# Gated linear attention with routed experts on one core: the decay matrices of chunks 2 to 5 from two 64x64 triangles and a product of two factors

## The chip, the cores and the metric

One core of a Trainium2 chip runs the whole program, in one launch. The metric is the device time of one execution in microseconds (us); lower is better. The engines are TensorE (PE in the profile, its weight loads PEld), VectorE (DVE), ScalarE (ACT), GpSimd (POOL) and SyncE (SP), whose queue issues most DMAs. Each works through its own instructions in program order; semaphores order them against each other.

## The reference, cut to what matters

```python
# attention: batch 4, heads 8, seq 768, head_dim 40
for t in range(S):
    m_new = np.maximum(f_gate[:, :, t] + m, i_gate[:, :, t])
    f_stab = np.exp(f_gate[:, :, t] + m - m_new)
    i_stab = np.exp(i_gate[:, :, t] - m_new)
    m = m_new
    C = f_stab * C + i_stab * np.einsum('bhd,bhe->bhde', vt, kt)
    n = f_stab * n + i_stab * kt
    h_tilde = np.einsum('bhde,bhe->bhd', C, qt)
    denom = np.maximum(np.abs(np.einsum('bhd,bhd->bh', n, qt)), 1.0)
    y[:, :, t] = sigmoid(o_gate[:, :, t]) * h_tilde / denom
# then 8 experts 320 -> 1024 -> 320, one per token (the best logit), weighted by its probability
# then one dense block 320 -> 2048 -> 320 for all 3072 tokens
```

The attention is a linear recurrence with a scalar decay `f_stab` per head and token. Over a chunk of 128 tokens it becomes a few matrix products, in which the weight of key token s for query token t is the product of the decays from s + 1 to t. That triangle of products, 128x128 for each head, is what the change computes in another way.

## The kernel before, in words

The attention is cut into 24 units: chunk c (128 tokens, 6 of them) by batch b (4 of them), unit u being chunk u // 4 and batch u % 4. All 8 heads of a batch are done at once. The loop over u is written out by hand, and what stands in the program first comes first on its engine; there is no planner in it.

For unit u the work is this. `fload` (L264) brings the chunk's decays of 8 heads, 1024 numbers, to all 128 partitions of `fb`. `scan` (L358) runs VectorE's scan over them, multiply and add with a shifted identity: row s of the result `pm` is the running product that starts at token s, which is the triangle. `scores_mm` (L392) makes the scores `sp` of 8 heads on TensorE, `scores_w` (L402) multiplies them by `pm` to `wm`, and `pv` (L453) multiplies `wm` by the values into `op`. `kweigh` (L383, GpSimd) weighs the keys by the last column of `pm`, and `state` (L407) makes of them the product `dC`, which `state_up` (L423, VectorE) adds to the state `Cst`, decayed by `state_decay` (L417, three instructions on ScalarE). `inter` (L437) multiplies the queries by the state. `epilogue1` and `epilogue2` join both parts in `num` and make the denominator `dn`; `finish` (L495) multiplies by the gate `sg` on GpSimd and leaves the token rows `x`. Two units later `route_t` (L503) transposes `x` (into `pr`, copied to `xT` by ScalarE), and `route_l` (L533) makes the logits, which VectorE copies to `logit_all`. `route_hot`, `route_rank` and `route_cnt` find, for 4 units at a time, the slot of each token with its expert; `scatter` (L613, GpSimd, from unit 10 on) writes the rows there.

On GpSimd the order in a unit is `sg` and `x` of unit u - 2, `vp_in` (the weighted values) of unit u + 1, `kw` of unit u + 1, a row scatter. On TensorE it is `sp` of u, `op` of u - 1, `pr` of u - 2, `dC` of u, `ip` of u, the logits of u - 2. In the last chunk (units 20 to 23) there is no `kw`, `dC`, `Cst` decay or update. From unit 10 on halves of expert weights are split into two parts beside it (ScalarE L105 and L118, VectorE L110, L111 and L121).

The gates of all 32 heads stand on 32 partitions. Chunks 0 and 1 are prepared at the start, chunks 2 to 5 in units 0 to 5 (`gates_m`, `gates_x`, `gates_exp_f`, `gates_z`, `gates_e`, `gates_pe`). `put_dec` writes the decays to DRAM, from where `fload` spreads them.

The attention is followed by the experts and the dense block, in which TensorE multiplies 128x128 weight blocks in fp32 split into two fp32r parts.

## Time and profile before

| | us |
|---|---|
| median of 3 runs (lowest, highest) | 760.16 (759.28, 760.32) |
| the profiled execution | 759.01 |
| its span, first to last instruction | 757.3 |

| engine | busy us | share of the span |
|---|---|---|
| TensorE (PE) | 712.0 | 94% |
| VectorE (DVE) | 538.7 | 71% |
| ScalarE (ACT) | 345.2 | 46% |
| GpSimd (POOL) | 232.4 | 31% |

The shares are means over two stages with different limits. The page's picture of the span in 40 slices of 18.9 us each shows VectorE at 8 to 9 tenths in the first ten slices (the attention) and at 4 to 7 after them, TensorE at 6 to 9 in the first ten and at 9 tenths or more in nearly all the others. A row of the order of time is an instruction, or several alike merged: its start, how long from the first start to the last end, engine, line, operation, what it writes from what, shapes and count; in brackets how long the engine stood idle before it and whose end released it.

### The profile page before, as it was taken

Reading aid. Unit: us, or ns where it says so; the run is one execution under the profiler, and the core shown is the slowest. Engines: PE = TensorE matmul, PEld = TensorE weight load, DVE = VectorE, ACT = ScalarE, POOL = GpSimd, SP = SyncE. Lnnn points to the kernel's source line nnn. Section 1 sums busy time; section 2 is a strip of 40 time slices with the busy share of each in tenths; the row PEclk is TensorE's granted clock in tenths of the full one; section 3 lists DMA queues with packets and bytes.
Section 4 is the critical chain, followed back from the end, with each engine's and each line's share of the span. In section 5 each row is a group of like instructions: output and inputs, shape, how many; then the busy total and the mean of one; then the engine's idle time right before and its main releaser. Section 6 shows DMA issues by size and latency. Waiting matters only on the chain.

```text
span 757.3 us, 13220 instructions
## 1 busy us (share of the span) xinstructions
PE 712.0 (94%) x4708; PEld 669.0 (88%) x4708; DVE 538.7 (71%) x1082; ACT 345.2 (46%) x806; POOL 232.4 (31%) x346
## 2 busy tenths in 40 slices
PE   7697888878999999999999999999999999999995
PEld 6697888878888999999998888998889988899994
DVE  7889999998499989898976765544544554445542
ACT  4344243332566666676645443333333343334442
POOL 4563476785343333455401003003003003002011
PEclk9889999999999999999999999999999999999998
DMA  6979887672559777877732121211211101101000
GB/s 188 314 244 300 265 268 237 205 256 77 165 198 234 234 203 188 233 209 232 250 82 80 27 59 46 42 33 40 40 41 36 37 26 35 43 1 46 11 19 18
DMA packets 69913, 99.57 MB, mean 131 GB/s; under 512 B 31218, under 2 KB 56082, under 8 KB 69842
## 3 DMA queue, kind: packets, MB, share of 16 engines
q1 hardware_dynamic: 66770, 90.79, 40.6%
q0 software_dynamic: 3072, 7.89, 2.9%
q8 instruction: 38, 0.62, 0.3%
q14 instruction: 33, 0.27, 0.1%
HBM read 77.53 MB, written 17.19 MB: 125 GB/s over the span
## 4 chain that ended last, share of the span: by engine, by line
issue 42%; PE 23%; POOL 5%; DVE 2%; DMA 1%; ACT 0%; POOLq 0%; SPq 0%; ACTq 0%
PE acc L1131 12%; PE hp L138 10%; POOL out_dram L1176 3%; POOL xr L1282 2%; PE xt L1055 1%; DMA xr<-y 1%; DVE w L121 0%; POOL gap L1178 0%; DVE hs L1105 0%; DVE xl L1057 0%; DVE w L111 0%; DVE fr L1200 0%; POOLq L1626 0%; DVE xl L1073 0%; ACT hs L1444 0%
## 5 line engine op out<-in xcount | busy, mean ns | idle before, releaser
L1131 PE MATMUL acc<-wout,hhl 128*128 128x320 f32 x1152 | 187.0, 309 | 0.0
L1131 PEld LDWEIGHTS acc<-wout,hhl 128*128 128x128 f32 x1152 | 175.9, 188 | 7.4
L1116 DVE TENSOR_TENSOR sg<-hp,sg 128x512 f32<-128x512 f32 (+1 forms) x112 | 68.8, 614 | 93.5 <-ACT sg L1115 93.1
L138 PE MATMUL hp<-xh,win 128*128 128x512 f32 (+1 forms) x560 | 131.0, 364 | 0.0
L1118 DVE TENSOR_TENSOR hhl<-sg,hhl 128x512 fp32r<-128x512 f32 (+1 forms) x112 | 71.3, 637 | 70.2 <-ACT hhl L1117 70.2
L1176 POOL DMA_INDIRECT out_dram<-o,tokd x24 | 24.0, 1001 | 312.4 <-ACT o L1160 308.7
L1115 ACT ACTIVATE sg<-hp 128x512 f32<-128x512 f32 (+1 forms) x112 | 60.4, 539 | 124.6 <-PE hp L138 124.6
L1131 PE MATMUL acc<-w,hs 128*128 128x320 f32 x636 | 104.9, 310 | 2.0 <-ACT hs L1104 1.0
L138 PEld LDWEIGHTS hp<-xh,win 128*128 128x128 f32 x560 | 93.9, 188 | 11.5 <-ACT xh L1321 0.2
L1131 PEld LDWEIGHTS acc<-w,hs 128*128 128x128 f32 x636 | 96.8, 188 | 4.4 <-DVE hs L1105 1.9
L1117 ACT CAST hhl<-sg 128x512 fp32r<-128x512 f32 (+1 forms) x112 | 62.6, 559 | 80.1 <-DVE sg L1116 80.1
L138 PE MATMUL hp<-xl,win 128*128 128x512 f32 (+1 forms) x336 | 85.7, 363 | 0.0
L110 POOL TENSOR_TENSOR w<-r,w 128x256 fp32r<-128x256 f32 x58 | 47.7, 824 | 106.6 <-ACT w L105 94.2
L138 PEld LDWEIGHTS hp<-xl,win 128*128 128x128 f32 x336 | 58.8, 189 | 10.9 <-DVE xl L1322 0.2
L138 PE MATMUL hp<-xh,w 128*128 128x440 f32 (+6 forms) x320 | 66.8, 338 | 0.0
L400 PE MATMUL sp<-qT,kblk 120*128 120x128 f32 x384 | 51.9, 292 | 11.9 <-DVE wm L405 11.9
L400 PEld LDWEIGHTS sp<-qT,kblk 120*128 120x128 f32 x384 | 48.2, 204 | 16.7 <-DVE wm L405 14.6
L360 DVE TENSOR_TENSOR_SCAN pm<-fb,ident_h 128x1024 f32<-128x1024 f32 x23 | 57.3, 2492 | 5.2 <-DMA fb<-dec 2.0
L138 PEld LDWEIGHTS hp<-xh,w 128*128 128x128 f32 x320 | 51.4, 189 | 1.7
L1104 ACT ACTIVATE hs<-hp 128x440 fp32r<-128x440 f32 (+6 forms) x64 | 30.2, 472 | 41.5 <-PE hp L138 40.1
L463 PE MATMUL op<-vp_in,wm 128*128 128x128 f32 (+1 forms) x368 | 44.6, 275 | 0.0
L463 PEld LDWEIGHTS op<-vp_in,wm 128*128 128x128 f32 x368 | 43.5, 194 | 0.0
(304 smaller groups left out, 1082.8 us busy)
## 6 DMA issues: line engine op xcount, KB each, us to landing
r<-in_w_dram SPq DMA_DIRECT2D x32, 704.0 KB
fb<-dec SPq DMA_DIRECT2D x23, 512.0 KB
kvo<-in_kvo_dram SPq DMA_DIRECT2D x24, 480.0 KB
c<-in_wio_dram SPq DMA_DIRECT2D x16, 704.0 KB
rows<-zt SPq DMA_DIRECT2D x8, 640.0 KB
qT<-in_qT_dram SPq DMA_DIRECT2D x24, 180.0 KB
xr<-y SPq DMA_DIRECT2D x5, 640.0 KB
kblk<-in_kT_dram SPq DMA_DIRECT2D x48, 60.0 KB
```

The lines of the kernel that those rows point to most:

```text
L110: eng.tensor_tensor(out=t[:, 3 * P:5 * P].rearrange("p (c f) -> p c f", c=2), in0=r1[:, 0:2], in1=hif[:, 0:2], op=ALU.subtract)
L138: nc.tensor.matmul(hp, a, b, start=(i == 0), stop=(i == len(seq) - 1))
L360: nc.vector.tensor_tensor_scan(out=pm[u].rearrange("p h t -> p (h t)"), data0=fb[u].rearrange("p h t -> p (h t)"), data1=ident_h.rearrange ...
L400: nc.tensor.matmul(sp[:, h - hs.start], kblk[u % NLD][0:KR, h // 3, h % 3, :], qT[u][0:KR, h // 3, :], start=True, stop=True)
L463: nc.tensor.matmul(ops[:, h * NW:h * NW + n], wm[u][:, h], vp_in[u % NLD][:, h * DV:h * DV + n], start=True, stop=True)
L1104: nc.scalar.activation(out=hh, in_=hp, func=AF.Relu)
L1115: nc.scalar.activation(out=sg, in_=hp, func=AF.Sigmoid, scale=1.702)
L1116: nc.vector.tensor_tensor(out=g, in0=hp, in1=sg, op=ALU.mult)
L1117: nc.scalar.copy(hh, g)
L1118: nc.vector.tensor_tensor(out=hl, in0=g, in1=hh.bitcast(F32), op=ALU.subtract)
L1131: nc.tensor.matmul(acc_t[blk][i], hl if j == 2 else hh, w[:, DM:2 * DM] if j == 1 else w[:, 0:DM], start=(first and j == 0), stop=(last an ...
L1176: sc = nc.gpsimd.indirect_dma_start(out=out, out_offset=bass.IndirectOffsetOnAxis(ap=tokd[:, ti:ti + 1], axis=0), in_=o[:, i], in_offset=None)
```

## The change

For chunks 2 to 5 (units 8 to 23) the triangle of 128 tokens is put together from three blocks of 64. `fload` brings the decays of the first 64 tokens to the upper 64 partitions of `fb` and those of the last 64 to the lower, so that one scan of 512 elements makes both triangles. It writes to a PSUM tile `tri`; ScalarE copies the first triangle into `pm` (L429). The square between them is a product of two factors, the decays from s to token 63 and those from token 64 to t, made on TensorE (`far_mm`, one product of K = 96: for 8 heads the factors' high parts and the low parts of each, against zeros for the other heads) into the upper half of the same PSUM tile; `far_out` copies square and second triangle into `pm` (L444). The gates therefore stand on 96 partitions, three copies of the 32 heads, each loaded by a DMA of its own.

The factors are made once: `masks` in unit 1, `factors` in `gates_e` in unit 4, `suffix` in two parts in units 5 and 6, and their spreading over heads and batches (`spread_b`, `spread_a`) at the ends of units 5 and 6. `far_mm` stands behind `inter` in a unit, `far_out` and `kweigh` behind `state_decay`. Besides, `pv` multiplies 96 columns at a time instead of 128, `pm` is two fixed tiles, and a later tile takes the place of a `wm` tile instead of a `pm` tile.

```diff
-        ig = ap1.tile([BH, S], F32, name="ig")
-        fg = ap1.tile([BH, S], F32, name="fg")
-        nc.sync.dma_start(out=fg, in_=f_gate.rearrange("b h s -> (b h) s"))
-        nc.sync.dma_start(out=ig, in_=i_gate.rearrange("b h s -> (b h) s"))
+        R3, HP, CH = 3 * BH, P // 2, 2
+        ig = ap1.tile([R3, S], F32, name="ig")
+        fg = ap1.tile([R3, S], F32, name="fg")
+        for t, g in ((fg, f_gate), (ig, i_gate)):
+            for a in range(3):
+                nc.sync.dma_start(out=t[a * BH:(a + 1) * BH], in_=g.rearrange("b h s -> (b h) s"))
...
+            else:
+                fb[u] = fb[u][:, 0:H * HP]
+                for a in range(2):
+                    src = dec[1][2 * (c - CH) + a, b * H:(b + 1) * H].rearrange("h t -> (h t)").unsqueeze(0)
+                    nc.sync.dma_start(out=fb[u][a * HP:(a + 1) * HP], in_=src.to_broadcast([HP, H * HP]))
...
+        def masks():
+            v = ident[0:R3, 0:R3].rearrange("k (a b h) -> k a b h", b=B, h=H)
+            nc.vector.tensor_reduce(out=hmask, in_=ident[0:R3, 0:R3].rearrange("k (a h) -> k h a", h=H), axis=AX.X, op=ALU.add)
+            nc.vector.tensor_reduce(out=bmask, in_=v.rearrange("k a b h -> k b a h"), axis=AX.XY, op=ALU.add)
+            for a in range(2):
+                nc.vector.tensor_copy(id2[a * HP:(a + 1) * HP],
+                                      ident[a * HP:(a + 1) * HP, a * HP:(a + 1) * HP].unsqueeze(1).to_broadcast([HP, H, HP]))
+        def suffix(second):
+            if not second:
+                nc.gpsimd.memset(facA[:, :, HP - 1:HP], 1.0)
+                nc.gpsimd.tensor_copy(facA[:, :, 0:HP - 1], fz[:, CH:NCH, 1:HP])
+            k = 8 if second else 1
+            while k < (HP if second else 8):
+                nc.vector.tensor_tensor(out=facA[:, :, 0:HP - k], in0=facA[:, :, 0:HP - k], in1=facA[:, :, k:HP], op=ALU.mult)
+                k *= 2
+            if not second:
+                return
+            nc.scalar.copy(fac["fa"], facA)
+            lo = slice(BH, 2 * BH)
+            nc.vector.tensor_tensor(out=fac["fa"][lo], in0=facA[lo], in1=fac["fa"][lo].bitcast(F32), op=ALU.subtract)
+        def factors():
+            late = est[:, CH:NCH, HP:P]
+            nc.scalar.copy(fac["fb"], late)
+            lo = slice(2 * BH, R3)
+            nc.vector.tensor_tensor(out=fac["fb"][lo], in0=late[lo], in1=fac["fb"][lo].bitcast(F32), op=ALU.subtract)
+            nc.vector.tensor_tensor(out=late, in0=late, in1=est[:, CH:NCH, HP - 1:HP].to_broadcast([R3, NCH - CH, HP]), op=ALU.mult)
+        def spread_a():
+            for b in range(B):
+                nc.scalar.mul(lhsA[:, b], fac["fa"].bitcast(F32), bmask[:, b:b + 1])
+        def spread_b(h0, h1):
+            for h in range(h0, h1):
+                nc.scalar.mul(rhsB[:, :, h], fac["fb"].bitcast(F32), hmask[:, h:h + 1])
...
         def scan(u):
-            pm[u] = wk.tile([P, H, P], F32, tag="pm", name="pm")
+            pm[u] = pmb[u % 2]
+            if units[u][1] >= CH:
+                t = tri_t[u] = ps_t.tile([P, H, HP], F32, tag="pt", name="tri")
+                nc.vector.tensor_tensor_scan(out=t.rearrange("p h t -> p (h t)"), data0=fb[u], data1=id2.rearrange("p h t -> p (h t)"),
+                                             initial=0.0, op0=ALU.mult, op1=ALU.add)
+                nc.scalar.copy(pm[u][0:HP, :, 0:HP], t[0:HP])
+                return
...
+        def far_mm(u):
+            b, c = units[u]
+            if c >= CH:
+                nc.tensor.matmul(tri_t[u][0:HP].rearrange("p h t -> p (h t)"), lhsA[:, b, c - CH],
+                                 rhsB[:, c - CH].rearrange("k h t -> k (h t)"), start=True, stop=True)
+        def far_out(u):
+            if units[u][1] >= CH:
+                nc.scalar.copy(pm[u][:, :, HP:P], tri_t.pop(u))
...
-                n = min(2, H - h) * NW
+                n = NW + NW // 2 if h < H - 1 else NW
...
                 if ok(u + 1):
                     vprime(u + 1)
-                    kweigh(u + 1)
+                    if units[u + 1][1] < CH:
+                        kweigh(u + 1)
...
                 inter(u)
+                if ok(u + 1):
+                    far_mm(u + 1)
...
                 state_decay(u)
+                if ok(u + 1) and units[u + 1][1] >= CH:
+                    far_out(u + 1)
+                    kweigh(u + 1)
```

The order on ScalarE in unit 11, before (`vp_in` is a column of the weighted values, `Cst` the state of a batch, `w` a split weight):

```order
L381 COPY vp_in_118<-ei_tok 128x8
L511 COPY xT<-pr 128x384 [waits PE_49]
L469 ACTIVATE sg<-kvo 128x320
L517 ACTIVATE sq,ss_all<-x 128x320 [waits Activation_49,Pool_49]
L421 ACTIVATE Cst_177<-Cst_177,gdec 120x123 [waits PE_49] x3
L118 CAST w<-r 128x320
```

and now, the same unit:

```order
L429 COPY pmb_140<-tri 64x8x64 [waits DVE_49]
L464 COPY vp_in_122<-ei_tok 128x8
L594 COPY xT<-pr 128x384 [waits PE_49]
L552 ACTIVATE sg<-kvo 128x320 [waits DMAHW1_49]
L600 ACTIVATE sq,ss_all<-x 128x320 [waits Activation_49,Pool_49]
L504 ACTIVATE Cst_191<-Cst_191,gdec 120x123 [waits PE_49] x3
L444 COPY pmb_140<-tri 128x8x64 [waits PE_49]
L118 CAST w<-r 128x320
```

Two copies have come in: the first triangle (L429) ahead of the unit's other work, square and second triangle (L444) behind the decays.

On GpSimd the order of the instructions stays, and what `kw` waits for changes. Before, from one row scatter to the next:

```order
L498 TENSOR_TENSOR sg<-sg,dn 128x320 [waits DVE_49,Activation_49]
L501 TENSOR_TENSOR x<-num,sg 128x320 [waits DMASW2_49,Pool_49]
L380 TENSOR_TENSOR vp_in_118<-kvo,ei_tok 128x8x40 [waits DMAHW5_49,PE_49]
L387 TENSOR_TENSOR kw<-kvo,pm 128x320 [waits DVE_49,PE_49]
L616 DMA rows<-x,slot_i 26624x320
```

and now:

```order
L581 TENSOR_TENSOR sg<-sg,dn 128x320 [waits DVE_49]
L584 TENSOR_TENSOR x<-num,sg 128x320 [waits DMASW2_49,Pool_49]
L463 TENSOR_TENSOR vp_in_122<-kvo,ei_tok 128x8x40 [waits DMAHW0_49,PE_49]
L470 TENSOR_TENSOR kw<-kvo,pmb_141 128x320 [waits Activation_49]
L699 DMA rows<-x,slot_i 26624x320
```

`kw` (L387, now L470) waited for VectorE, whose scan made `pm`; it waits for ScalarE, whose copy L444 makes it.

On VectorE, unit 6, behind the denominators, now (before, `logit_all` came straight behind `dn`):

```order
L570 SCALAR_TENSOR_TENSOR dn<-num 128x8
L572 TENSOR_SCALAR dn<-dn 128x8
L574 RECIPROCAL dn<-dn 128x8
L360 TENSOR_TENSOR facA<-facA 96x4x56
L360 TENSOR_TENSOR facA<-facA 96x4x48
L360 TENSOR_TENSOR facA<-facA 96x4x32
L366 TENSOR_TENSOR fa<-facA,fa 32x256
L625 COPY logit_all<-r 128x8 x2
```

The second part of `suffix` has come in between the denominators and the copy of the logits.

## Rows read from the trace of the kernel before

**Rows 1.** Busy us (instructions) of each engine, granted clock, DMA, in two stretches

```profile
core 0: us, PE busy (x) PEld busy (x) DVE busy (x) ACT busy (x) POOL busy (x), PEclk, DMA share, GB/s
37.00:42.00 5.00, 4.71 (x22) 4.71 (x23) 4.90 (x8) 1.50 (x4) 4.37 (x4) 0.51 1.03 337
120.00:140.00 20.00, 17.66 (x157) 17.09 (x155) 19.61 (x39) 7.76 (x26) 14.97 (x16) 1.00 0.83 259
```

**Rows 2.** Order of time, TensorE, unit 16

```profile
126.50 2.05 PE L400 MATMUL sp<-qT,kblk 120*128 120x128 f32 x16 [1.09 <-DVE wm L405]
128.39 1.90 PE L463 MATMUL op<-vp_in,wm 128*128 128x128 f32 x16
130.12 0.31 PE L507 MATMUL pr<-ident,x 128*128 128x128 f32 x1
...
131.72 0.42 PE L538 MATMUL r<-enT,xT 128*128 128x128 f32 x2
...
133.36 2.05 PE L400 MATMUL sp<-qT,kblk 120*128 120x128 f32 x16 [0.77 <-DVE wm L405]
```

**Rows 3.** Order of time, VectorE, units 15 and 16

```profile
122.72 2.60 DVE L360 TENSOR_TENSOR_SCAN pm<-fb,ident_h 128x1024 f32<-128x1024 f32 x1
...
128.25 0.84 DVE L435 SCALAR_TENSOR_TENSOR Cst<-dC,mask,Cst 120x123 f32<-120x123 f32 x3
...
129.41 2.78 DVE L360 TENSOR_TENSOR_SCAN pm<-fb,ident_h 128x1024 f32<-128x1024 f32 x1
```

**Rows 4.** Order of time, TensorE, the scores of units 7, 10, 19, 23

```profile
61.51 1.95 PE L400 MATMUL sp<-qT,kblk 120*128 120x128 f32 x16
...
82.84 2.05 PE L400 MATMUL sp<-qT,kblk 120*128 120x128 f32 x16 [0.50 <-DVE wm L405]
...
148.43 2.05 PE L400 MATMUL sp<-qT,kblk 120*128 120x128 f32 x16 [0.35 <-DVE wm L405]
...
177.55 1.95 PE L400 MATMUL sp<-qT,kblk 120*128 120x128 f32 x16
```

**Rows 5.** Groups by line and shape, VectorE: busy us, mean ns of one

```profile
L110 DVE TENSOR_TENSOR win<-ex,win 128x256 fp32r<-128x256 f32 x16 | 6.7, 416 | 0.0
L111 DVE TENSOR_TENSOR win<-ex,win 64x128 fp32r<-64x128 f32 x16 | 4.6, 289 | 0.2
...
L373 DVE TENSOR_TENSOR_SCAN pm<-f,ident_h 128x512 f32<-128x512 f32 x2 | 2.3, 1194 | 0.0
```

**Rows 6.** Order of time, ScalarE, unit 16

```profile
130.69 0.48 ACT L511 COPY xT<-pr 128x384 f32<-128x384 f32 x1 [4.58 <-PE pr L509]
...
131.89 0.96 ACT L421 ACTIVATE Cst<-Cst,gdec 120x123 f32<-120x123 f32 x3
132.75 0.50 ACT L105 CAST w<-r 128x384 fp32r<-128x384 f32 x1
```

**Rows 7.** Order of time, GpSimd, units 15 and 16

```profile
125.47 0.74 POOL L387 TENSOR_TENSOR kw<-kvo,pm 128x320 f32<-128x320 f32 x1 [2.29 <-PE r L540]
126.36 1.01 POOL L616 DMA_INDIRECT rows<-x,slot_i  x1 [0.15 <-issue]
...
128.45 0.72 POOL L498 TENSOR_TENSOR sg<-sg,dn 128x320 f32<-128x320 f32 x1 [0.99 <-DVE dn L491]
129.25 0.81 POOL L501 TENSOR_TENSOR x<-num,sg 128x320 f32<-128x320 f32 x1
```

**Rows 8.** Order of time, a scan and a row scatter in unit 19

```profile
151.81 2.61 DVE L360 TENSOR_TENSOR_SCAN pm<-fb,ident_h 128x1024 f32<-128x1024 f32 x1
...
152.42 2.82 POOL L616 DMA_INDIRECT rows<-x,slot_i  x1
```

**Rows 9.** Order of time, VectorE's scan and TensorE's logits in unit 6

```profile
56.13 2.29 DVE L360 TENSOR_TENSOR_SCAN pm<-fb,ident_h 128x1024 f32<-128x1024 f32 x1 [1.30 <-POOL vp_in L380]
...
60.77 0.46 PE L538 MATMUL r<-enT,xT 128*128 128x128 f32 x2 [2.19 <-DVE logit_all L542]
```

**Rows 10.** Order of time, TensorE, the scores of unit 4

```profile
37.29 3.79 PE L400 MATMUL sp<-qT,kblk 120*128 120x128 f32 x16 [3.33 <-DVE wm L405]
```

**Rows 11.** Order of time, VectorE, the first scan over the gates

```profile
3.97 0.41 DVE L275 TENSOR_TENSOR_SCAN mm<-fg,ig 32x128 f32<-32x128 f32 x1 [0.20 <-DMA ig<-in_i_gate_dram]
```

More of the change, by code (lines that the diff above doesn't have):

```diff
@@ L195 @@
         nc.vector.tensor_copy(ident_h, ident.unsqueeze(1).to_broadcast([P, H, P]))
+        id2 = ap1.tile([P, H, HP], F32, name="id2")
+        hmask = ap1.tile([R3, H], F32, name="hmask")
+        bmask = ap1.tile([R3, B], F32, name="bmask")
+        fac = {n: ap1.tile([R3, NCH - CH, HP], F32R, name=n) for n in ("fa", "fb")}
+        facA = ap1.tile([R3, NCH - CH, HP], F32, name="facA")
+        lhsA = ap1.tile([R3, B, NCH - CH, HP], F32R, name="lhsA")
+        rhsB = ap1.tile([R3, NCH - CH, H, HP], F32R, name="rhsB")
+        pmb = [ap1.tile([P, H, P], F32, name=f"pmb{i}") for i in range(2)]
         tri = ap1.tile([P, P], F32, name="tri")
@@ L301, in gates_z @@
         def gates_z(c0, c1):
+            if c0 >= CH:
+                at = lambda t: t.rearrange("k c (a t) -> k c a t", t=HP)[:, c0:c1, :, 0:1]
+                nc.vector.tensor_copy(at(fd), at(fz))
+                nc.vector.memset(at(fz), 0.0)
+                return
             if c0:
@@ L313, in gates_e @@
             n = c1 - c0
+            if c0 >= CH:
+                factors()
             gd = wk.tile([BH, n, B * G], F32, tag="gd", name="gd")
@@ L323, in gates_pe @@
             for i in range(n):
-                nc.tensor.transpose(pg[:, 2 * i * BH:(2 * i + 1) * BH], ist[:, c0 + i], ident[0:BH, 0:BH])
-                nc.tensor.transpose(pg[:, (2 * i + 1) * BH:(2 * i + 2) * BH], est[:, c0 + i], ident[0:BH, 0:BH])
+                nc.tensor.transpose(pg[:, 2 * i * BH:(2 * i + 1) * BH], ist[0:BH, c0 + i], ident[0:BH, 0:BH])
+                nc.tensor.transpose(pg[:, (2 * i + 1) * BH:(2 * i + 2) * BH], est[0:BH, c0 + i], ident[0:BH, 0:BH])
             g0 = 2 * n * BH
@@ L709, in early_x @@
             if c == 0:
-                for n, tag in (("h", "fb"), ("l", "pm")):
+                for n, tag in (("h", "fb"), ("l", "wm")):
                     t = wk.tile([P, H, P], F32R, tag=tag, name="xe" + n).rearrange("p h t -> p (h t)")
@@ L869 @@
                     gates_pe(2, NCH)
+                if u in (5, 6):
+                    suffix(u == 6)
+                if u == 1:
+                    masks()
                 if ok(u + 1):
                     vprime(u + 1)
-                    kweigh(u + 1)
+                    if units[u + 1][1] < CH:
+                        kweigh(u + 1)
                 if u == 3:
```

37 lines of the change are left out of this document (23 added, 14 removed).

## The prediction, made before the changed kernel ran

> **What bounds the kernel now.** I read the busy time by stage first, then the order of time of each engine in one unit of the attention, then who waited for whom, and last the tensor engine's starts along the stage. From 120 to 140 us VectorE is busy for 19.61 of 20 us, TensorE for 17.66, GpSimd for 14.97 and ScalarE for 7.76 [rows 1]. The unit whose scores start at 126.50 lasts until 133.36, 6.86 us [rows 2]; both of these starts waited (1.09 and 0.77 us) for VectorE's product `wm`. TensorE's own work in it, from 126.50 to the end of the three routing pairs (131.72 plus 6 x 0.11, the step of the `op` passes), is 5.9 us. So VectorE sets the pace, and TensorE stands 0.8 to 1 us behind it. VectorE's largest instruction there is the scan, 2.60 and 2.78 us [rows 3]. After the attention TensorE works without a gap to the end, so a microsecond won or lost in the attention is one at the end.
>
> **The change part by part.** Four stretches of the score starts [rows 4] carry the sum: up to 61.51 (unit 7), 61.51 to 82.84 (units 7 to 9, 21.33 us), 82.84 to 148.43 (10 to 18, 65.59 us), 148.43 to 177.55 (19 to 22, 29.12 us).
>
> The scan. The 16 scans of units 8 to 23 go from 1024 to 512 elements. Two scans of 512 from PSUM took 1194 ns each [rows 5], so I take 1.2 us, and the product with its identity no less: VectorE loses at least 2.60 - 1.20 = 1.4 us a unit. To PSUM as a destination no row speaks; the bounds are 1.1 and 1.5 us. VectorE's unit falls from 6.86 to about 5.45 us, below TensorE's, so something else is late next. The product `wm` now also awaits the second copy, which is done 2 us ahead of it.
>
> TensorE. It gains one product of 512 columns a unit (between 0.2 us, if one pass streams twice as fast as the two-pass 128-column ones at 0.11 each, and 0.45), and 14 of the 16 `op` passes narrow from 128 to 96 columns: the 16 passes take (130.12 - 128.39) / 16 = 0.108 us each, so this gives between nothing and 14 x 0.027 = 0.38 us. I take both as cancelling: 5.9 us a unit, 5.3 without the state product (0.57) in the last chunk.
>
> The new chain. `kweigh` moves from behind the scan to the unit's end, behind ScalarE's second copy. On GpSimd the row scatter, then `sg` and `x` of the unit before, queue behind it, and TensorE's transpose `pr` of the next unit waits for that `x`. That closes a loop through four engines, from one `pr` to the next. In terms: `pr` to `xT` 130.69 - 130.12 = 0.57 and `xT` to the decays 131.89 - 130.69 = 1.20 [rows 2, 6]; decays to ScalarE's next instruction 132.75 - 131.89 = 0.86, the second copy's place; that copy, 128x512, between the 0.50 of a 128x384 cast and four thirds of it, 0.67, taken as 0.55 [rows 6]; hand-over to `kw` 125.47 - (122.72 + 2.60) = 0.15 [rows 3, 7]; `kw` to the scatter 0.89, scatter 1.01, 0.1 to `sg`, `sg` to `x` 0.80, `x` 0.81 [rows 7]. Sum 6.94 us. In units 7 to 9 no scatter stands there (they begin at unit 10), which takes away 0.89 + 1.01 + 0.1 and puts 0.80 back: 5.74 us.
>
> The port. A scan and GpSimd's work on SBUF shut each other out: the scan at 151.81 ended at 154.42, and the scatter issued at 152.42 took 2.82 us, 0.82 past that end, where one takes 1.01 [rows 7, 8]. Before, what is held up is mostly `vp_in`, which nobody awaits. In the loop it is what everybody awaits. Behind `pr`, VectorE's state update may start when the decays are done, 0.57 + 1.20 + 0.96 = 2.73; the scan follows 129.41 - 128.25 = 1.16 later, at 3.9. `kw` runs from 3.33 to 4.07, and the scatter would start at 4.22. So the scan gets its turn when `kw` ends, holds until 5.25, and the scatter ends at 6.07 instead of 5.23: 0.82 more. In about 7 of 9 units; in the two with the routing counters in front of it VectorE comes later. In units 7 to 9 it is `sg` that waits, about 0.95.
>
> The Trainium skill, "SBUF — State Buffer", section "Who interferes with whom", has the general rule: a VectorE instruction with two SBUF inputs contends with GpSimd instructions that read SBUF, whole instruction against whole instruction. It adds, as inferred, that descriptor generation needs only the write side, by which a scatter would not wait for such a scan; the trace disagrees with that part (2.82 against 1.01 us) [rows 7, 8]. By the inferred part the sum would be 7 x 0.82 = 5.7 us smaller.
>
> Units 10 to 18: 9 x 6.94 + 7 x 0.82 = 68.2 against 65.59, **+2.6**; bounds 62.5 (no collision) and 9 x 8.0 = 72.
>
> Units 7 to 9: one at TensorE's pace (6.0) and two at 5.74 + 0.95: 19.4 against 21.33, **-1.9**; bounds 17.7 and 21.
>
> Units 19 to 22: `kweigh` ends with unit 19, the loop is open. Unit 19 takes 7.0; then TensorE needs 5.3 and GpSimd two scatters, `sg`, `x` and `vp_in`, 2 x 1.2 + 3 x 0.8 = 4.8, to 6.0 if a scan holds it up: 5.6 twice; unit 22 carries a ranking and the last unit's `ip`, whose PSUM slot now comes free behind `xT` (0.6): 7.2. Sum 25.4 against 29.12, **-3.7**; bounds 23.5 and 27.5.
>
> Set-up on VectorE. A two-input product of 256 elements takes 416 ns, of 128 elements 289 [rows 5]. In unit 4 `factors` adds a ScalarE copy that VectorE waits for (0.5) and two of 256: 1.3 us. Unit 5 adds three of about 250: 1.2. Unit 6 adds 224, 192 and 128 elements (1.0), a copy to wait for (0.5) and one of 256 (0.4): 1.9. All of it stands ahead of the copy `logit_all`, for which TensorE waited 2.19 us before it could go on to the scores of 61.51 [rows 9]. Of these 4.4 us, 1.30 fall into VectorE's own wait ahead of the scan at 56.13: **+3.1**, bounds 1.5 and 4.5. The masks in unit 1 (1 us) I cost at nothing: VectorE soon stands waiting for loads; without that cover they cost that microsecond. ScalarE's twelve scalings have room in its 7.8 of 20 us.
>
> TensorE then stands still for 2.2 + 3.1 = 5.3 us. A standstill of 3.33 us ahead of 37.29 went with scores of 3.79 instead of 2.05 us and a granted clock of 0.51 (the 1.2 GHz level) in 37 to 42 [rows 1, 10]. The same here would cost 0 to 3 us; I take **+1.0**.
>
> Start. Six gate loads stand where two did, four more SP issues; the first gate scan waited for `ig` [rows 11]. It comes some 1.8 us later, but the identity copies now run ahead of it and the loads of unit 1's decays were awaited anyway: **+0.3**, bounds 0 and 1.8. The `fb` loads halve in bytes and double in issues; no wait on the path hangs on them from unit 8 on, so nothing.
>
> Sum: 3.1 + 1.0 + 0.3 - 1.9 + 2.6 - 3.7 = **+1.4 us**. On the profiled execution's 759.01 us (span 757.3 and 1.7 around it) that is 760.4; the median of the runs is 760.16, 1.15 above that execution, so a median of about **761.5** is forecast.
>
> **The rivals.** *A, the scatter gets in first.* If the second copy is shorter or the hand-over quicker by 0.3 us, the scatter has begun before the scan takes its turn, and 7 x 0.82 = 5.7 us go: 755.8. For it: the margin between 3.9 and 4.2 us is thin, and both ends of it hang on instructions that no row shows. Against it: `kw` itself ends only after the scan is due, and the scan then goes next. It decides from a copy under about 0.25 us on, or a state update that starts 0.3 us later. It ends faster than before.
>
> *B, the set-ups and the clock cost more.* The products of units 5 and 6 collide with GpSimd's `sg` and `x` as the scan does, and TensorE's standstill brings the low clock for a whole unit: +1.4 for the collisions and +2 for the clock, 765. For it: the standstill is longer than any that kept the clock; against it: idle times of VectorE further on take up some.
>
> *C, the set-ups are hidden.* Load waits like the 1.30 us take up all of them: -3.1, 758.4. For it: the stage up to unit 7 is full of loads; against it: the wait for `logit_all` stands behind that one.
>
> **How the numbers follow.** What a measurement can tell from no change is 0.2%, 1.5 us. Forecast 0.55, with 758 to 766 as its own range: slower 0.27, same 0.20, faster 0.08. A 0.22: faster 0.19, same 0.03. B 0.13: slower 0.12, same 0.01. C 0.10: faster 0.05, same 0.05. Together faster 0.32, same 0.29, slower 0.39. The range reaches down to A's loop without any collision and TensorE's gains (754) and up past B (766.5).
>
> **What would show it.** In the profile after: scans of 512 at about 1.2 us; `kw` waiting for ScalarE; `pr` waiting for `x` in units 10 to 18, VectorE no longer at 98%; scatters of 1.8 to 2 us under the scans; score starts 7.5 us apart there, 5.5 to 6 in units 20 and 21; the scores of unit 7 about 4 us later than 61.51, after a standstill of 5 us. I am wrong if units 10 to 18 run at 6 us, which would mean that GpSimd's chain has slack that I don't see, or if unit 7 starts where it did.

## The result, and the profile after

| | us |
|---|---|
| before, median of 4 runs on the same chip (lowest, highest) | 759.72 (759.28, 760.32) |
| after, median of 4 runs (lowest, highest) | 769.11 (768.84, 771.83) |
| ratio, 95% interval | 1.0131 [1.0107, 1.0156] |
| span of the profiled execution, before and after | 757.3 and 767.5 |

The kernel is slower by 1.3%, where 761.5 us (754 to 766.5) were forecast. The first view to read is again TensorE's order of time at the starts of the scores: units 6, 7, 10, 19 and 23 of the kernel after, against [rows 4] and, for unit 6, the row of before that stands below it.

```profile
53.72 1.95 PE L483 MATMUL sp<-qT,kblk 120*128 120x128 f32 x16
...
71.23 2.66 PE L483 MATMUL sp<-qT,kblk 120*128 120x128 f32 x16
...
91.50 1.95 PE L483 MATMUL sp<-qT,kblk 120*128 120x128 f32 x16
...
159.71 1.95 PE L483 MATMUL sp<-qT,kblk 120*128 120x128 f32 x16
...
186.00 1.95 PE L483 MATMUL sp<-qT,kblk 120*128 120x128 f32 x16
```

```profile
52.37 1.95 PE L400 MATMUL sp<-qT,kblk 120*128 120x128 f32 x16
```

They cut the span into stages, whose differences add up to the 10.2 us of the two spans:

| stage | before | after | change | forecast |
|---|---|---|---|---|
| up to the scores of unit 6 | 52.37 | 53.72 | +1.35 | +4.4 for this row and the next |
| unit 6 | 9.14 | 17.51 | +8.37 | (start 0.3, set-up 3.1, clock 1.0) |
| units 7 to 9 | 21.33 | 20.27 | -1.06 | -1.9 |
| units 10 to 18 | 65.59 | 68.21 | +2.62 | +2.6 |
| units 19 to 22 | 29.12 | 26.29 | -2.83 | -3.7 |
| from the scores of unit 23 on | 579.75 | 581.50 | +1.75 | 0 |

One unit holds most of the loss. TensorE ahead of unit 7, then ScalarE and VectorE in the same stretch, all of after:

```profile
60.54 0.27 PE L592 MATMUL pr<-ident,x 128*128 128x128 f32 x1
...
67.23 0.80 PE L621 MATMUL r<-enT,xT 128*128 128x128 f32 x2 [6.41 <-ACT xT L594]
```

```profile
53.83 1.69 ACT L382 ACTIVATE rhsB<-fb,hmask 96x256 fp32r<-96x256 f32 x4
66.30 0.41 ACT L364 CAST fa<-facA 96x256 fp32r<-96x256 f32 x1 [10.78 <-DVE facA L360]
66.61 0.20 ACT L464 COPY vp_in<-ei_tok 128x8 f32<-128x8 f32 x1
66.71 0.47 ACT L594 COPY xT<-pr 128x384 f32<-128x384 f32 x1
```

```profile
56.56 2.15 DVE L360 TENSOR_TENSOR facA<-facA 96x252 f32<-96x252 f32 x3
58.63 0.15 DVE L625 COPY logit_all<-r 128x8 f32<-128x8 f32 x1
...
59.88 2.27 DVE L431 TENSOR_TENSOR_SCAN pmb<-fb,ident_h 128x1024 f32<-128x1024 f32 x1
62.07 1.19 DVE L488 TENSOR_TENSOR wm<-sp,pmb 128x1024 f32<-128x1024 f32 x1
...
64.23 1.98 DVE L360 TENSOR_TENSOR facA<-facA 96x224 f32<-96x224 f32 x3
```

ScalarE has nothing to do for 10.78 us: the copy `fa` of `suffix` is next in its program and waits for VectorE's last product, which comes behind the scan, `wm` and the denominators of the unit. Behind it stand the `xT` copies of two units, whose transposes were done at 58.1 and 60.8. TensorE waits for the first of them for 6.41 us. In [rows 9] the wait at this place was the one for `logit_all`, of 2.19 us, and only one routing (0.74 us) stood behind it; now two routings and `ip` do, 4.0 us from 67.23 to 71.23. Of the 9.7 us by which unit 7 is late, 6.5 are the later end of the wait (67.23 against 60.77) and 3.3 this work behind it: a routing and `ip` that ran ahead of the wait before (57.11 to 58.58), and the clock. The granted clock falls to 0.50, the 1.2 GHz level: before, the same two routings and `ip` took 2.2 us at 1.00, so the clock costs some 1.8 of the 4.0 us (an estimate from these rows). The busy time of the engines by stretch (columns as in [rows 1]), after:

```profile
60.00:70.00 10.00, 3.59 (x22) 3.35 (x21) 6.62 (x11) 3.27 (x11) 2.99 (x4) 0.62 0.14 41
70.00:80.00 10.00, 10.00 (x84) 9.94 (x84) 7.46 (x26) 7.11 (x21) 1.06 (x2) 0.86 0.73 221
120.00:140.00 20.00, 17.89 (x159) 17.26 (x158) 16.74 (x42) 10.63 (x33) 12.05 (x16) 1.00 0.70 208
```

The third row answers to the second of [rows 1]: VectorE is down from 19.61 to 16.74 of 20 us, and TensorE hardly busier than it was. The loop that the forecast spoke of can be read in units 15 and 16. GpSimd, then TensorE's transposes, then scans of VectorE (the first rows of GpSimd and of VectorE are of units 14 and 15), all of after (answering to [rows 7, 8]):

```profile
124.94 1.61 POOL L584 TENSOR_TENSOR x<-num,sg 128x320 f32<-128x320 f32 x1
...
130.80 1.01 POOL L699 DMA_INDIRECT rows<-x,slot_i  x1 [0.16 <-issue]
...
137.09 0.74 POOL L470 TENSOR_TENSOR kw<-kvo,pmb 128x320 f32<-128x320 f32 x1 [2.48 <-ACT pmb L444]
137.98 1.82 POOL L699 DMA_INDIRECT rows<-x,slot_i  x1 [0.15 <-DMA rows<-x,slot_i]
139.80 0.09 POOL L701 MEMSET gap<- 1x1 f32 x1
139.85 0.73 POOL L581 TENSOR_TENSOR sg<-sg,dn 128x320 f32<-128x320 f32 x1
140.66 0.94 POOL L584 TENSOR_TENSOR x<-num,sg 128x320 f32<-128x320 f32 x1
```

```profile
133.79 0.33 PE L590 MATMUL pr<-ident,x 128*128 128x128 f32 x1 [0.98 <-POOL x L584]
...
141.66 0.33 PE L590 MATMUL pr<-ident,x 128*128 128x128 f32 x1 [1.66 <-POOL x L584]
```

```profile
124.49 1.48 DVE L427 TENSOR_TENSOR_SCAN tri<-fb,id 128x512 f32<-128x512 f32 x1
...
131.12 1.22 DVE L427 TENSOR_TENSOR_SCAN tri<-fb,id 128x512 f32<-128x512 f32 x1
...
137.76 1.22 DVE L427 TENSOR_TENSOR_SCAN tri<-fb,id 128x512 f32<-128x512 f32 x1
```

From one `pr` to the next are 7.87 us, and each waits for `x`. The scatter, which begins 0.22 us after the scan, takes 1.82 us. In the unit before it begins 0.32 us ahead of the scan: it takes 1.01 us and the scan its 1.22, although they overlap for 0.69. Six of the nine units from 10 to 18 last 7.72 to 7.88 us, the other three 7.08 to 7.18. Of the six, four (12, 13, 16 and 17) have such a scatter of 1.82 us; in the other two (14 and 18), where the scan comes later behind a ranking, it is `x` that begins during the scan and takes 1.61 us instead of 0.81. Of the three, unit 10 has no scatter in its stretch, and in 11 and 15 the scatter begins first (by 0.06 and 0.32 us).

### The profile page after: what moved, and what is told of

It reads as the page before. It is cut to its first block, busy times and chain, and to the rows that moved or that the text cites. A ratio compares the mean times of both kernels' runs of the same rounds, so it can differ in the third digit from the quotient of the medians.

```text
span 767.5 us, 13326 instructions
## 1 busy us (share of the span) xinstructions
PE 716.1 (93%) x4724; PEld 672.3 (88%) x4724; DVE 529.6 (69%) x1095; ACT 367.4 (48%) x852; POOL 230.8 (30%) x348
## 4 chain that ended last, share of the span: by engine, by line
issue 41%; PE 23%; POOL 5%; DVE 2%; DMA 1%; POOLq 0%; ACT 0%; SPq 0%; ACTq 0%
PE acc L1228 11%; PE hp L138 10%; POOL out_dram L1273 3%; POOL xr L1379 2%; PE xt L1152 1%; DMA xr<-y 1%; DVE w L121 0%; POOL gap L1275 0%; DVE hs L1202 0%; DVE xl L1154 0%; DVE w L111 0%; DVE fr L1297 0%; POOLq L1723 0%; DVE xl L1170 0%; PE xt L1168 0%
## 5 line engine op out<-in xcount | busy, mean ns | idle before, releaser
L546 PE MATMUL op<-vp_in,wm 128*128 128x96 f32 (+1 forms) x368 | 44.2, 273 | 0.1
L138 PE MATMUL hp<-xl,w 128*128 128x440 f32 (+6 forms) x192 | 42.9, 331 | 0.0
```

Source lines behind the costliest of these rows:

```text
L138: nc.tensor.matmul(hp, a, b, start=(i == 0), stop=(i == len(seq) - 1))
L546: nc.tensor.matmul(ops[:, h * NW:h * NW + n], wm[u][:, h], vp_in[u % NLD][:, h * DV:h * DV + n], start=True, stop=True)
```

## The experiments

All of them change the kernel after; the ratio is to the kernel before, run on the same chip. "Unit 7" is the start of its scores in the profiled execution.

| run | median us | ratio, 95% interval | unit 7 | units 10 to 18 |
|---|---|---|---|---|
| after | 769.11 | 1.0131 [1.0107, 1.0156] | 71.23 | 68.21 |
| fa copy late | 766.46 | 1.0093 [1.0057, 1.0128] | 67.33 | 68.21 |
| + suffix behind the logits | 762.68 | 1.0055 [1.0037, 1.0073] | 65.30 | 69.72 |
| fa copy late, suffix on GpSimd | 761.94 | 1.0039 [1.0019, 1.0059] | 65.52 | 69.84 |
| no suffix products | 766.64 | 1.0098 [1.0074, 1.0123] | 64.55 | 69.01 |
| scatter first | 758.63 | 1.0009 [0.9993, 1.0024] | 71.53 | 61.29 |
| far product early | 766.44 | 1.0098 [1.0078, 1.0118] | 71.02 | 66.25 |
| scatter first, suffix on GpSimd in units 4, 5 | 755.71 | 0.9948 [0.9929, 0.9967] | 65.48 | 61.69 |
| the same, far product in the middle | 754.51 | 0.9942 [0.9925, 0.9958] | 66.33 | 60.13 |
| the same, op passes of 128 columns | 754.79 | 0.9944 [0.9927, 0.9960] | 66.16 | 60.13 |
| far product in the middle, suffix in units 5, 6 | 755.29 | 0.9947 [0.9933, 0.9960] | 64.46 | 59.44 |
| + input gates from a second queue | 754.75 | 0.9939 [0.9924, 0.9954] | 63.16 | 60.09 |
| fa copy late, unit 22 filled | 767.11 | 1.0105 [1.0079, 1.0132] | 66.45 | 69.18 |
| no suffix products, unit 22 filled | 762.84 | 1.0041 [1.0020, 1.0063] | 64.79 | 68.04 |
| second queue, unit 22 filled | 755.18 | 0.9939 [0.9924, 0.9954] | 63.25 | 60.71 |

How far a single execution can be trusted is seen where the program is the same up to unit 7: its scores start at 71.23, 71.53 and 71.02 in the kernel after, the scatter first and the far product early, at 67.33 and 66.45 with the fa copy late (without and with unit 22 filled), at 64.55 and 64.79 in the two without products. The last column holds stretches at a granted clock of 0.50 in some rows, each in a unit that is longer by it: units 13 and 15 with the suffix behind the logits, 18 with the late copy and the suffix on GpSimd, 12 without products, 12 with the fa copy late and unit 22 filled, 16 without products and with unit 22 filled, 14 with the far product early.

**The fa copy late.** Theory: ScalarE's queue and, behind it, VectorE's set-up products ahead of `logit_all` hold up unit 7. Rivals: VectorE alone, or ScalarE alone.

```diff
-            nc.scalar.copy(fac["fa"], facA)          # in suffix(True), middle of unit 6
+                if u == 6:                           # behind state_decay(6)
+                    factor_a()
```

> ScalarE's copy fa (and VectorE's product of its low part) is moved from the middle of unit 6 to the unit's end, nothing else. Theory 1 (ScalarE's queue): in the changed kernel that copy waits 10.78 us for VectorE's suffix products and shuts in the two xT copies behind it, for which TensorE stands 6.4 us; with it moved the xT copies run at about 61, and what is late next is the copy logit_all behind the same products (about 66.3), so the scores of unit 7 start at about 67 instead of 71.23, and the time is about 765 us (769.1 before). Theory 2 (VectorE's own time alone): ScalarE's wait is hidden behind VectorE's, the scores of unit 7 stay at 70 to 71 and the time at 768 to 770. Theory 3 (ScalarE's queue is all of it): the scores of unit 7 come at about 63, the time is about 761.

Unit 7 starts at 67.33, as the first theory had it. ScalarE makes both `xT` at 57.58 and 60.39, and TensorE now waits for VectorE's copy, in this kernel:

```profile
65.91 0.77 PE L621 MATMUL r<-enT,xT 128*128 128x128 f32 x2 [4.32 <-DVE logit_all L625]
...
67.33 2.81 PE L483 MATMUL sp<-qT,kblk 120*128 120x128 f32 x16
```

The time falls by less than unit 7's start (766.46, expected 765).

**The products elsewhere.** First behind the copies of the logits, then on GpSimd behind `kw`:

```diff
-                if u in (5, 6):                      # behind pv, epilogue2
-                    suffix(u == 6)
...
+                if u in (5, 6):                      # behind route_l, route_hot
+                    suffix(u == 6)
                 state_decay(u)
```

> As the run with the late fa copy (scores of unit 7 at 67.33), and VectorE's suffix products of units 5 and 6 behind the copies of the logits in their units instead of ahead of them. Theory (what is left of the delay ahead of unit 7 is VectorE's second suffix part, 2.0 us, for which TensorE waits at logit_all): the scores of unit 7 start at 65 to 65.5, and of the 2 us 1 to 2 stay in the time: 763 to 765.5. Rival (the delay is VectorE's sum of work since unit 5, wherever it stands): the scores of unit 7 at 67 again, or 65 with those of unit 9 no earlier than 81.4, and the time as before, 765 to 767.

65.30, as expected, and 762.68 us, 0.3 below the range. The fall of the time is not the products alone: in the profiled executions unit 22 went from 12.35 to 7.60 us (the clock, see below), and units 13 and 15 lost time to the clock here.

```diff
-                nc.vector.tensor_tensor(out=facA[:, :, 0:HP - k], ...
+                nc.gpsimd.tensor_tensor(out=facA[:, :, 0:HP - k], ...
```

> As the run with the late copy, and the six suffix products of units 5 and 6 on GpSimd behind its kw, instead of on VectorE. If VectorE's 4.1 us of these products are the other part of the delay: the scores of unit 7 at 63 to 65, time 761 to 763. If the products are hidden anyway or GpSimd becomes late with them (about 0.6 us each, 3.6 us in two units in which it is busy for less than half of the time): as the run before, 765 or more.

65.52 and 761.94 us, inside the time, half a microsecond outside the start. On GpSimd the first three products last 3.97 us, and `x`, queued behind them, makes TensorE wait for 3.58:

```profile
56.48 3.97 POOL L360 TENSOR_TENSOR facA<-facA 96x252 f32<-96x252 f32 x3
60.41 0.72 POOL L581 TENSOR_TENSOR sg<-sg,dn 128x320 f32<-128x320 f32 x1
61.21 0.81 POOL L584 TENSOR_TENSOR x<-num,sg 128x320 f32<-128x320 f32 x1
```

**No suffix products.** The loop of `suffix` is taken out, so the far square is not what it should be.

> The changed kernel without the six suffix products of units 5 and 6 (4.1 us of VectorE; the factor of the first 64 tokens is then not the product that it should be, and the far square is another); the fa copy and all else stand where they did. Theory (all of the delay ahead of unit 7 beyond what is there at unit 6 comes from these products, half of it by the time they take on VectorE, half by the fa copy that shuts in the xT copies behind them): the scores of unit 7 at 62.5 to 63.5 (71.23 in the changed kernel), time 760 to 762. Rival (the fa copy's place costs by itself, since it waits for VectorE's queue with or without them): the scores of unit 7 at 66 to 67, time 764 to 766.

Unit 7 starts at 64.55, 6.7 us earlier: between the theory (at most 63.5) and the rival (at least 66). The time (766.64) lies above the ranges of both; it fell by 2.5 us only. Most of the rest went into unit 22, which lasted 8.23 us in the kernel after and 11.77 here. TensorE in unit 22, then the stretches, of the run without products (its lines are one lower):

```profile
172.74 1.95 PE L482 MATMUL sp<-qT,kblk 120*128 120x128 f32 x16
176.32 0.22 PE L670 MATMUL r<-oh_all,ones 128*128 128x24 bf16 x3 [1.59 <-DVE oh_all L650]
180.49 2.85 PE L532 MATMUL ip<-Cst,qT 120*128 120x123 f32 x12 [0.57 <-ACT xT L593]
```

```profile
168.00:176.00 8.00, 6.73 (x61) 6.59 (x61) 7.68 (x16) 2.95 (x9) 7.47 (x12) 1.00 0.60 200
176.00:186.00 10.00, 9.12 (x56) 8.62 (x56) 6.06 (x17) 3.02 (x9) 5.48 (x11) 0.66 0.21 84
```

Behind a standstill of 1.59 us the granted clock is at 0.50 (1.2 GHz) for some 7 of the 10 us of the second stretch. The run with the late fa copy has the same at the same place (1.59 us, then 0.52 in the mean of 10 us, unit 22 of 12.35 us); the kernel after stands for 0.95 us there and keeps 1.00. So the standstill was filled:

```diff
                 if batch:
+                    if u == 22:
+                        keep_warm(dC.rearrange("p g f -> p (g f)"), 8)
                     route_rank(batch)
```

> As the run without the six suffix products (the far square is another for that), with the same 8 products of the identity in unit 22. If the clock drop hid the gain: unit 22 at 8 to 8.5 us instead of 11.77, time 760.5 to 763 (766.64; what may be left is the drop in unit 13, 2 us); otherwise 765.5 to 767.5.

> As the run with the late fa copy, with 8 products of the identity into the unused state tile on TensorE ahead of the ranking of unit 22 (about 1.8 us, where TensorE stood 1.59 us for VectorE's oh_all). If the clock drop of unit 22 hid the gain: unit 22 lasts 8 to 8.5 us instead of 12.35, clock 1.00 there, time 762 to 763.5 (766.46). If the gain is hidden by something else: 765.5 to 767.5.

Without the products, unit 22 falls to 8.91 us (8 to 8.5 expected), its clock stays at 1.00, and the time falls to 762.84 (ratio 1.0041 against 1.0098), as expected. This execution has its drop in unit 16 (9.49 us) where the one without the filling has it in unit 12. TensorE and the same stretch of that run:

```profile
172.37 1.95 PE L482 MATMUL sp<-qT,kblk 120*128 120x128 f32 x16
174.16 1.95 PE L84 MATMUL dC<-ident 128*128 128x128 f32 x16
...
178.98 1.57 PE L532 MATMUL ip<-Cst,qT 120*128 120x123 f32 x12 [0.57 <-ACT xT L593]
```

```profile
176.00:186.00 10.00, 9.20 (x84) 8.71 (x83) 7.97 (x19) 3.69 (x11) 6.03 (x10) 1.00 0.22 84
```

With the late fa copy, unit 22 falls to 8.91 too, but the time does not (767.11, expected 762 to 763.5): here the theory missed. Its profiled execution (766.14), 1.6 us shorter than that of the run without the filling, shows where unit 7's gain goes. Against the kernel after, unit 7 starts 4.8 us earlier; units 7 to 9 take 0.9 us more, units 10 to 18 1.0 (a drop in unit 12, 9.50 instead of 7.87 us), units 19 to 22 0.8 (the filled unit 22 is 0.7 longer than the 8.23 us that it took there), and the end 1.0 less. The mean granted clock of the four timed executions says part of the rest: 765.45 and 766.14 us at 0.988, 768.09 and 770.15 at 0.980 and 0.979. In which units these two lost it is not shown, and the two at 0.988 lie above the range as well.

> The version with the suffix products on GpSimd in units 5 and 6, the far product behind the state product, the scatter ahead of kw and the input gates from a second queue (754.75; no clock drop behind unit 9 in its trace), with the same 8 products in unit 22. If its runs fall into that clock drop at times: 752.5 to 754. If never, the products only cost what they do beyond the standstill of 0.7 us: 755 to 756.

On the version that had no drop behind unit 9 in its trace, the filling changes nothing (0.9939 both).

**The loop.** Scatter ahead of `kw`, then the far product, copy and `kw` early:

```diff
-                for i in range(0 if u < US else 1 if u < NU - 5 else 2):   # at the unit's end
-                    if pend:
-                        scatter(pend.pop(0))
...
+                for i in range(0 if u < US else 1 if u < NU - 5 else 2):
+                    if pend:
+                        scatter(pend.pop(0))
                 state_decay(u)
```

> From the changed kernel: GpSimd's row scatter stands ahead of kw in the unit, not behind it; ScalarE's and VectorE's order is as it was. Theory (the loop pr, xT, decays, second copy, kw, scatter, sg, x, pr sets the pace of units 10 to 18, 6.94 us and 0.82 for the port): without the scatter in it the loop is 5.74 us, 6.7 where sg meets the scan, so the score starts stand 6.0 to 6.7 us apart (7.58 in the changed kernel), and the time falls by 8 to 14 us, to 755 to 761. Rival (VectorE or the loads set the pace): 7.3 to 7.6 us apart, time within 2 us of 769.

Units 10 to 18 fall from 68.21 to 61.29 us, 6.81 each, a tenth above the range, and the time by 10.5 us, as expected: the loop was the bound of these units. Of the 10.8 us between the two profiled spans 6.9 are theirs, 1.1 come from units 7 to 9 and 2.9 from the part behind the scores of unit 23, which the theory does not speak of. What is left of the loop is the `sg` that meets the scan of 133.01 to 134.23:

```profile
132.99 1.75 POOL L581 TENSOR_TENSOR sg<-sg,dn 128x320 f32<-128x320 f32 x1
134.82 0.80 POOL L584 TENSOR_TENSOR x<-num,sg 128x320 f32<-128x320 f32 x1
```

```diff
                 if ok(u + 1):
+                    far_mm(u + 1)                    # behind pv, ahead of the transposes
                     vprime(u + 1)
-                    if units[u + 1][1] < CH:
-                        kweigh(u + 1)
+                    far_out(u + 1)
+                    kweigh(u + 1)
```

> From the changed kernel: the far product stands behind the op passes on TensorE, the second copy behind it on ScalarE ahead of xT, kw behind vp_in as it was before the change. This takes the second copy, kw and the scatter out of the loop (kw no longer waits for the decays). Theory of the loop: TensorE's own 5.9 to 6.1 us sets the pace of units 10 to 18, the time falls by 11 to 15 us, to 754 to 758. Rival (VectorE or the loads set the pace): 7.3 to 7.6 us a unit, within 2 us of 769. Second rival: ScalarE's second copy now waits for the far product ahead of xT and makes xT late by up to 1 us; then 6.5 to 7 us a unit, 760 to 764.

66.25 us, and 766.44: the first theory missed. The loop over GpSimd is open, but the far product, which writes where the first triangle is read, now waits for ScalarE's copy of it ahead of the transposes, 0.23 to 1.18 us in units 10 to 18. The second rival (6.5 to 7 us a unit) is nearer: unit 14 had a clock drop (10.02 us, where unit 18, with a ranking too, took 8.42); with that taken off, the nine units stand at some 7.2 us, an estimate. The first row is of the unit with the drop:

```profile
126.69 0.69 PE L439 MATMUL tri<-rhsB,lhsA 96*64 96x512 f32 x1 [0.84 <-ACT pmb L429]
...
134.94 0.45 PE L439 MATMUL tri<-rhsB,lhsA 96*64 96x512 f32 x1 [0.41 <-ACT pmb L429]
```

**Both together.** The edits of the products (now ahead of `kw` in units 4 and 5) and of the scatter in one kernel; then the far product behind `state`, ahead of `inter`; then that with the 128 columns of before; then the products in units 5 and 6; then a second queue for the loads.

> Late fa copy; the suffix products on GpSimd in units 4 and 5, ahead of kw, where GpSimd waits 4.70 us for the scan; and the scatter ahead of kw. If the two causes (ScalarE's and VectorE's queue ahead of unit 7; the loop over GpSimd) are separate, their gains add: scores of unit 7 at 62.5 to 64.5, units 10 to 18 at 6.8 us as in the run with the scatter ahead alone, time 749 to 752, faster than the kernel before the change by 6 to 10 us. If they are one and the same slack, no better than the scatter ahead alone: 757 to 759.

755.71: faster than before, but 3.7 us above the range. The two gains stand side by side (unit 7 at 65.48, units 10 to 18 at 6.85 us each), so they are two causes. What is missing: unit 22 has the drop (11.28 us), and in unit 5 a new queue formed: GpSimd's products stand ahead of its index constants `e_i`, for which a ScalarE copy waits that stands ahead of the `fb` copy, for which VectorE waits. In the run with the far product in the middle these are, on GpSimd, ScalarE and VectorE:

```profile
45.74 2.76 POOL L360 TENSOR_TENSOR facA<-facA 96x252 f32<-96x252 f32 x3
```

```profile
49.31 0.20 ACT L743 CAST e<-e_i 128x8 f32<-128x8 int32 x1 [3.59 <-POOL e_i L739]
```

```profile
51.40 0.78 DVE L373 TENSOR_TENSOR fb<-est,fb 32x256 fp32r<-32x256 f32 x1 [3.28 <-ACT fb L371]
```

> As the run before, and the far product behind the state product on TensorE (ahead of ip), the second copy behind xT and sg on ScalarE and kw behind it, so that kw no longer waits for the decays. Theory (in the run with the scatter ahead the loop is still what binds where sg meets the scan, 7.2 us, and TensorE elsewhere, 6.4): kw comes 1.5 to 2 us sooner, sg runs ahead of the scan, units 10 to 18 at 6.2 to 6.5 us, time 2 to 5 us below the run before: 745 to 749. Rival (the collisions only move to another instruction, or TensorE waits for the triangle's copy as in the run with the far product behind op): within 1.5 us of it.

754.51, 5.5 us above the range and 1.2 below the run before, within the 1.5 of the rival. Units 10 to 18 take 6.68 us each, not 6.2 to 6.5. Three of them are at 6.00 us, where TensorE never waits, from this row to the next:

```profile
134.33 1.95 PE L483 MATMUL sp<-qT,kblk 120*128 120x128 f32 x16
140.33 1.95 PE L483 MATMUL sp<-qT,kblk 120*128 120x128 f32 x16
```

In units 11, 12 and 15 the far product waits 0.43, 0.47 and 1.27 us for ScalarE's copy of the first triangle, as the rival had it, and in units 14 and 18 the ranking waits 0.59 and 0.58 us for `oh_all`. The queue in unit 5 is still there.

```diff
-                n = NW + NW // 2 if h < H - 1 else NW
+                n = min(2, H - h) * NW
```

> As the run with the far product behind the state product, but the op passes multiply 128 columns at a time as before the change, not 96. If a pass's time goes by its columns, each of 14 passes a unit takes up to 0.027 us more, 0.38 us a unit, and with TensorE as the bound in some 10 to 16 units the time rises by 3 to 6 us. If a pass takes the time of its weight load (128 rows in both), nothing changes: the op passes take 1.90 us a unit in both, the times agree within 1.5 us.

No difference, 754.79 against 754.51, and both units 10 to 18 at 60.13. The op line's instructions (minimum, median and maximum in ns) with 96 columns, then with 128:

```profile
L546 PE MATMUL op<-vp_in,wm x368: 248/275/329, 16.9 to 177.6; 128*128 128x96 f32 x161, 128*128 128x64 f32 x23
```

```profile
L546 PE MATMUL op<-vp_in,wm x368: 222/275/421, 18.0 to 178.1; 128*128 128x128 f32 x161, 128*128 128x64 f32 x23
```

> As the run with the far product behind the state product, but the suffix products on GpSimd one unit later, in units 5 and 6, each part ahead of kw, where GpSimd waited 4.70 and 3.00 us for the scan. In the two runs with them in units 4 and 5, the first part (2.76 us) stood ahead of GpSimd's index constants of unit 4, for which ScalarE and through it VectorE's factors waited 3.59 and 3.28 us, and the scores of unit 6 came at 57.9 to 58.8 with the clock at 0.66. If that is the reason, they come at 53.5 to 54 here, those of unit 7 at 63 to 64.5, and the time is 751 to 753. If GpSimd's products delay kw or x as much there, the scores of unit 7 stay at 65.5 to 66.5 and the time at 754 to 755.

The scores of units 6 and 7 come where they were expected (53.89, 64.46), the time does not: 755.29. So the queue was the reason for the late units 6 and 7, but the time does not show it. The gain of 1.7 us at unit 23 is lost behind it. From there to the end are 581.0 us, where the run with the far product in the middle needs 578.6; 1.1 of them are a wait for VectorE's `xel` in the first expert, as in the kernel after.

> As the run with the suffix products in units 5 and 6, and the three loads of the input gates issued from ScalarE's queue beside the forget gates' from SP's. If the 1.4 us by which the first gate scan is late (5.32 against 3.97) come from the six issues one behind the other on SP, about 1 us of it returns: first gate scan at 4.2 to 4.5, time 0.5 to 1.3 us below the run beside it. If the bytes or the first kblk loads set it, no change, within 0.5 us.

The first gate scan still waits for the loads, and longer (5.84 us), though all six are issued by 2.2 us here and by 3.5 in the kernel after; so the issues on SP were not it. Unit 7 starts 1.3 us earlier all the same. The time (754.75 against 755.29) is not clear of the spread of either run (752.99 to 755.75 and 754.12 to 756.25):

```profile
5.84 0.42 DVE L293 TENSOR_TENSOR_SCAN mm<-fg,ig 96x128 f32<-96x128 f32 x1 [2.07 <-DMA ig<-in_i_gate_dram]
```

## Why the prediction was wrong

Between the span's +10.2 us and the forecast's +1.4 are 8.8 us: 5.3 of them arise up to unit 7, 0.8 in units 7 to 9, 0.9 in units 19 to 22 and 1.75 behind the scores of unit 23.

*Set-up (+3.1) and clock (+1.0): this step failed.* Unit 7 came 9.7 us late, where set-up, clock and start were to make 4.4. The prediction asked of the copy `fa` only what VectorE loses by waiting for it (0.5 us), not what stands behind it on ScalarE; "ScalarE's twelve scalings have room in its 7.8 of 20 us" was a sum of busy time where an order was asked. The late copy shows that part: 3.9 of the 9.7 us (4.8 in the execution with unit 22 filled). The wait that the prediction lengthened, the one for `logit_all`, was overtaken by another, for `xT`, which stands one routing and `ip` earlier on TensorE. The clock's part is the smaller one: some 1.8 us, the estimate above, against 1.0. The Trainium skill, "PSUM — Partial Sum Buffer", section "Engine vs sequencer instructions", has the rule in a word: the queues of ScalarE, VectorE and GpSimd are strict FIFO. The rows agree: an `xT` copy whose input was done at 60.8 ran at 67.45.

The second part is the size of the products. Six of them were priced at 2.2 us, after 416 ns for 256 elements and 289 for 128 [rows 5]; they took 2.15 + 1.98 = 4.1. Two ran at 366 and 336 ns, the four that fell beside GpSimd's `sg` and `x` at 781 to 896. This is what rival B said of them, and the price it gave (+1.4) was somewhat low (four times 0.45 to 0.53, 1.9 together). Without the products, the copy in its place, unit 7 starts 6.7 us earlier: copy and products share the loss, and the copy (at 55.95 in that run, without a wait) costs little where it has nothing to wait for. Of the 3.0 us by which unit 7 is still later than before, 1.7 are there at unit 6.

*Start (+0.3).* Not decided. The first gate scan came at 5.32 instead of 3.97, about as expected, and units 4 and 5 start 1.45 and 0.8 us later than before; but in five executions whose program is the same up to there (the kernel after, the fa copy late without and with unit 22 filled, the scatter first, the far product early) unit 5 starts anywhere from 45.51 to 47.37, against 45.59 in the one of before.

*Scan, far product, op passes.* Right: scans of 512 to PSUM took 1.22 us; the far product 0.43, at the upper bound; the narrower op passes nothing, at the lower bound, which is seen only where TensorE is the bound. Its own unit is 6.00 us, not 5.9.

*The chain and the port in units 10 to 18 (+2.6).* The mechanism is right, and the number (+2.62) is so in part by luck. The terms of unit 15's loop: `pr` to `xT` 0.59, to the decays 1.20, to the second copy 0.86, to `kw` 0.65, to the scatter 0.89, to `sg` 1.87 (forecast 1.01 + 0.1 + 0.82), to `x` 0.81, to `pr` 1.00 (0.81). Without a collision the loop takes 7.16 to 7.18 us from `pr` to `pr` (6.94 forecast), with one 7.72 to 7.87 (7.76 forecast), and it collides in six units, not seven; the two differences cancel. The two units with a ranking, which were to be free of it, collide through `x`; in two others the scatter gets in first, by 0.06 and 0.32 us, which is rival A's condition, so A came in part. The scatter ahead of `kw` shows that the loop was the bound. "A scan and GpSimd's work on SBUF shut each other out" is too strong for the scatter: in [rows 8] and in these four units the scan came first, and where the scatter began first neither took longer: 1.01 us in unit 15 and once in the kernel before (at 173.34, 0.23 us ahead of a scan), 1.18 in unit 11, as the first scatter of the kernel before without a scan (1.17). On the inferred part of the rule that the prediction took from the Trainium skill, "SBUF — State Buffer", section "Who interferes with whom", that descriptor generation needs only the write side: the scatters of 1.82 us speak against it, those of 1.01 us beside a scan for it, so these runs don't refute it; what in a scatter waits is not shown.

*Units 7 to 9 (-1.9) and 19 to 22 (-3.7).* Right in sign, 0.8 and 0.9 short: units 7 and 8 took 6.96 and 6.95 us (in units 7 and 9 it is `x`, at 1.60 us, that meets the scan, and not `sg`), and unit 22 took 8.23 instead of 7.2, of which 0.95 is a wait for `oh_all`.

*"A shift in the attention is one at the end."* Nearly: from the scores of unit 23 to the end it was 581.5 us instead of 579.75, with 1.15 us of wait for `xel`, a product of VectorE. The traces fall into two groups: seven, the kernel after among them, have this wait of 1.10 to 1.15 us and take 579.9 to 581.5 us; nine, before among them, have none and take 578.5 to 579.75. What decides between the two was not followed. VectorE has less room there than the section on the profile before says: the page has it at 8 or 9 tenths in most slices of the second ten, and at 4 to 7 only behind them.

Open: in which units the timed executions of the late fa copy with unit 22 filled lose the rest of what unit 7 gains, and what decides on the wait for `xel`.

## What to carry to other kernels

For each instruction that an edit adds and that waits for another engine, read what stands behind it on its own engine, not only who waits for its result: a copy of 0.41 us held up ScalarE for 10.78. A set-up that is done once still costs what its place in four program orders makes of it; with the same copies and products on the same engines unit 7 started 9.7 us late in one order and 3.8 in another, and 1.7 with the products on GpSimd and the gate loads on two queues. And where a chain closes from unit to unit, taking one instruction out of it can be worth more than making the busiest engine faster: here the scan, shorter by some 1.4 us a unit, left units 10 to 18 2.6 us longer, and the scatter, put ahead of `kw`, made them 6.9 us shorter.
